# Segment sums on VectorE instead of TensorE, and one mean V moved into the first phase, in a two-part sequence kernel

## The chip, the cores and the metric

The kernel runs on one core of a Trainium2 chip. The metric is the device time of one execution in microseconds; lower is better. Each kernel was run several times, and beside runs of the kernel before on the same chip. The spans in the profiles are about 1.7 us shorter than the run times (1241.5 us of span against 1243.15 us for the same run of the kernel before).

## The reference

Two independent parts read inputs of 2048 positions and 1024 channels, and their outputs are put side by side.

```python
def _A_ref(x, ...):                     # a diagonal state space model
    Bu = jnp.einsum('bld,pd->blp', x + 0j, B_bar)
    for t in range(L):
        h = Lam_bar[None, :] * h + Bu[:, t, :]
    ...
def _B_ref(x, mem0, Wq, Wk, Wv, Wo, seg_len):   # attention by segments of 32, with a memory of 8 rows
    for s in range(n_seg):              # 64 segments, 32 heads of 128
        xs = x[:, s * seg_len:(s + 1) * seg_len, :].copy()
        h = jnp.concatenate([mem, xs], axis=1)
        v = jnp.einsum('btd,dhe->bhte', h, Wv)
        ...                             # q, k, softmax, output projection
        mem = o[:, :M, :].copy()        # the memory of the next segment
```

The memory makes part B sequential. The kernel avoids that with a first guess of every segment's memory: attention with equal weights, that is the mean of x over the segment (xbar), times Wv (the "mean V"), times Wo. A test on the chip raises a flag where the guess is not good enough, and a general path then runs.

## The kernel before

The engines have short names: `PE` is TensorE, `V` is VectorE, `S` is ScalarE (ACT), `G` is GpSimd. The profile calls VectorE DVE.

In the **first phase** (up to about 348 us) TensorE alternates between one step of part A (16 matmuls into psU) and one V piece of part B (32 matmuls into psP). There are 32 steps and 32 V pieces; after some steps there is no V piece. VectorE does the work of the steps. ScalarE copies a_g for the steps, makes part of their tables, and takes every V piece out of psP:

```python
    def stage1(self, pc, tb):           # one step of part A
        ...
        u = k.ps("U", (128, 2, TB))     # two psU buffers
        ...                             # 16 matmuls into u
        V.tensor_tensor(pr[:], u[:]..., view(t3, ...), ALU.mult)
        V.tensor_tensor(w, w, pr[:, :, 1, :], ALU.add)
        for j in range(2):
            V.tensor_tensor_scan(w[:, j, :], rb, w[:, j, :], ...)
            S.activation(g[:, j, :], w[:, j, :], ACT.Copy)     # ACT waits for the scan
        ...                             # GpSimd: the carry to the next step
        V.tensor_tensor(n[:], g[:]..., view(r3, ...), ALU.mult)  # DVE waits for a_g
        V.tensor_tensor(h[:], n[:, :, 0, :], n[:, :, 1, :], ALU.add)
```

The sums over the segments came from TensorE: 128 small matmuls of x rows with an indicator matrix, and VectorE scaled them out of PSUM.

```python
    def sum_x(self, tmp):
        ...                             # x rows loaded again, 128 at a time
        p = k.ps("R")
        for t in range(TT):             # TT = 16
            xr = xrs.pop(t)
            for c in range(KC):         # KC = 8
                o = c * NSEG + 4 * t
                k.PE.matmul(p[:, o:o + 4], xr[:, c * 128:(c + 1) * 128], k.ind[:], start=True, stop=True)
            load(t + 4)
            yield
        ...                             # xbar = p / L, three VectorE instructions
```

The loop of the first phase places them, and the mean V of a head block (`og`, 32 matmuls of 128x63 from Wv and xbar) comes after the last V piece of that block, for blocks 3 to 7. Blocks 2, 0 and 1 follow in the second phase:

```python
            for kind, pc, q in order[1:]:
                ...
                if kind == "v":
                    b.v_x(pc, q, wv[pc])           # one V piece
                    if q == 3:
                        if pc >= 3:
                            b.og(pc, wv[pc])       # needs xbar
                        n = (pc + 2) if pc + 2 < PC else (2, 0)[pc + 2 - PC]
                        wv[n] = b.load_wv(n)
                    continue
                ...
                if n == 1:
                    next(sx)
                if n >= 3:
                    for _ in range(2):
                        next(sx, None)             # two of the 16 groups of sums
                a.stage1(pc, q)                    # one step of part A, number n
                if q == 2 and pc + 1 < PC:
                    a.tables(pc + 1)               # tables: DVE and ACT by turns
```

TensorE's instructions of this phase stay in the order of the program (`keep_in_program_order`), so a matmul that waits holds up everything behind it.

Of the kernel before, what the change touches and what calls it, by code (L numbers as in the profile page):

```python
# [8 lines left out]
FP32 = mybir.dt.float32  # L9
BF16 = mybir.dt.bfloat16  # L10
I32 = mybir.dt.int32
ACT = mybir.ActivationFunctionType
ALU = mybir.AluOpType
AX = mybir.AxisListType
# [10 lines left out]
PC = 8; TB = 512; NB = 4  # L25
# [72 lines left out]
def consts(k):  # L98
    nc, V, G = k.nc, k.V, k.G
    c = k.cst  # L100
    k.ident = c.tile([128, 128], BF16, name="ident")
    G.memset(k.ident[:], 1.0)
    G.affine_select(out=k.ident[:], in_=k.ident[:], compare_op=ALU.is_equal, fill=0.0, base=0,
                    pattern=[[-1, 128]], channel_multiplier=1)
    k.ones = c.tile([128, 1], BF16, name="ones")
    V.memset(k.ones[:], 1.0)
    k.hpb = c.tile([128, 1], FP32, name="hpb")
    k.hpe = c.tile([128, 1], FP32, name="hpe")
    V.memset(k.hpb[:], HALF_PI)
    k.S.activation(k.hpe[:], k.hpb[:], ACT.Exp)  # L110
    k.ind = c.tile([128, 4], BF16, name="ind")
    G.memset(k.ind[:], 0.0)
    for j in range(4):
        G.memset(k.ind[32 * j:32 * j + 32, j:j + 1], 1.0)


def masks(k):
# [45 lines left out]
class PartA:  # L163
# [97 lines left out]
        for i, w in enumerate((self.Cim, self.Cre)):  # L261
            self.k.SP.dma_start_transpose(self.CT[:, i, :, cols], w[cols, :])

    def stage1(self, pc, tb):

        k = self.k; V, S, G, PE = k.V, k.S, k.G, k.PE
        if tb == 0:
            self.carry = None
        t3, r3 = self.tabs
        u = k.ps("U", (128, 2, TB))  # L270
        for i in range(2):
            for c in range(KC):
                PE.matmul(u[:, i, :], self.bt[:, i, c, :], self.xT[:, c, tb * TB:(tb + 1) * TB], start=(c == 0), stop=(c == KC - 1))
        pr = self.wp.tile([128, 2, 2, TB], FP32, name="a_pr", bufs=2)
        V.tensor_tensor(pr[:], u[:].unsqueeze(1).to_broadcast([128, 2, 2, TB]),  # L275
                        view(t3, [[TB + 1, 2], [TB + 1, 2], [1, TB]]), ALU.mult)
        w = pr[:, :, 0, :]
        V.tensor_tensor(w, w, pr[:, :, 1, :], ALU.add)
        rb = self.rr[:, pc:pc + 1].to_broadcast([128, TB])
        ini = self.carry  # L280
        g = self.wp.tile([128, 2, TB], BF16, name="a_g", bufs=2)
        for j in range(2):
            V.tensor_tensor_scan(w[:, j, :], rb, w[:, j, :], 0.0 if ini is None else ini[:, j:j + 1], ALU.mult, ALU.add)  # L283
            S.activation(g[:, j, :], w[:, j, :], ACT.Copy)
        if tb < NB - 1:
            nx = self.wp.tile([128, 2], FP32, name="a_nx", bufs=2); tt = self.wp.tile([128, 2], FP32, name="a_tt", bufs=2)
            for j in range(2):
                G.tensor_scalar(tt[:, j:j + 1], w[:, j, TB - 1:TB], t3[:, 1, TB:TB + 1], None, ALU.mult)  # L288
                G.tensor_scalar(nx[:, j:j + 1], w[:, 1 - j, TB - 1:TB], t3[:, 2 - 2 * j, TB:TB + 1], None, ALU.mult)
            G.tensor_tensor(nx[:], nx[:], tt[:], ALU.add)  # L290
            self.carry = nx
        n = self.wp.tile([128, 2, 2, TB], BF16, name="a_n", bufs=1)
        h = self.wp.tile([128, 2, TB], BF16, name="a_h", bufs=2)
        V.tensor_tensor(n[:], g[:].unsqueeze(1).to_broadcast([128, 2, 2, TB]), view(r3, [[TB, 2], [TB, 2], [1, TB]]), ALU.mult)
        V.tensor_tensor(h[:], n[:, :, 0, :], n[:, :, 1, :], ALU.add)
        k.SP.dma_start(self.hs[tb][:, pc, :, :], h[:])
# [48 lines left out]
class PartB:  # L345
# [77 lines left out]

    def sum_x(self, tmp):

        k = self.k
        xrs = {}

        def load(t):
            if t < TT:  # L430
                xrs[t] = tmp.tile([128, D], BF16, name="b_xr", bufs=4)
                k.SP.dma_start(xrs[t][:], self.x[0][t * 128:(t + 1) * 128, :])
        for t in range(4):
            load(t)
        yield
        p = k.ps("R")
        for t in range(TT):
            xr = xrs.pop(t)
            for c in range(KC):
                o = c * NSEG + 4 * t  # L440
                k.PE.matmul(p[:, o:o + 4], xr[:, c * 128:(c + 1) * 128], k.ind[:], start=True, stop=True)
            load(t + 4)
            yield
        pv = p[:].rearrange("p (c s) -> p c s", c=KC)
        ms = tmp.tile([128, KC], FP32, name="b_ms", bufs=1)
        k.V.tensor_reduce(ms[:], self.m0T[:], AX.X, ALU.add)
        k.V.tensor_scalar(self.xbar[:], pv, 1.0 / L, None, ALU.mult)
        k.V.tensor_tensor(ms[:], ms[:], pv[:, :, 0], ALU.add)
        k.V.tensor_scalar(self.xbar[:, :, 0], ms[:], 1.0 / L, None, ALU.mult)
        yield  # L450

    def load_wv(self, hb):
# [108 lines left out]
    def v_mem(self, hb, w=None):  # L561
        k = self.k
        w = w or self.load_wv(hb)
        p = k.ps("P")
        for h in range(4):
            for c in range(KC):
                k.PE.matmul(p[:, h * NM:(h + 1) * NM], w[:, c, h * 128:(h + 1) * 128], self.memT[:, c, :], start=(c == 0), stop=(c == KC - 1))
        vm = self.vmp.tile([128, 4, 128], BF16, name="b_vm", bufs=1)
        k.copy("v", vm[:, :, 0:NM], p[:, 0:4 * NM].rearrange("p (h n) -> p h n", h=4))
        if hb > 1:  # L570

            k.V.memset(vm[:, :, NM:128], 0.0)  # L572
            k.SP.dma_start(self.vmt[hb][:], vm[:].rearrange("p h n -> p (h n)"))
            yield
            s = self.next_st()[:].rearrange("p i h e -> p (i h e)")[:, 0:576].rearrange("p (h e) -> p h e", h=4)
            k.V.memset(s[:, :, E:EW], 1.0)
            for h in range(4):
                k.SP.dma_start_transpose(s[:, h, 0:E], self.vmt[hb][:, h * 128:(h + 1) * 128])
            yield
            k.SP.dma_start(self.vx[hb][64:64 + NMX, :].rearrange("n (h e) -> n h e", h=4), s[0:NMX, :, 0:EW])  # L580
            self.store_t(hb, s[:, :, 0:EW])
            yield
        yield
        pt = k.ps("P", (128, 1024), BF16)
        for h in range(4):
            k.PE.transpose(pt[0:NM, h * 128:(h + 1) * 128], vm[:, h, 0:NM], k.ident[:])
        st = self.next_st()
        k.copy("v", st[0:NM, 0, :, 0:E], pt[0:NM, 0:512].rearrange("p (h e) -> p h e", h=4))
        sv = st[:, 0, :, :].rearrange("p h e -> p (h e)")
        k.SP.dma_start(self.vx[hb][64:64 + NMX, :], sv[0:NMX, :])  # L590
        self.store_t(hb, st[:, 0, :, :])
        yield
# [427 lines left out]
def kernel_main(tc, A_x, A_Lre, A_Lim, A_Bre, A_Bim, A_Cre, A_Cim, A_logdt, A_Dskip, B_x, B_mem0, B_Wq, B_Wk, B_Wv, B_Wo, out,  # L1020
                force=False, dbg=None):
    with ExitStack() as ctx:
        k = K(tc, ctx)
        k.dbg = dbg
        nc = k.nc
        a = PartA(k, A_x, A_Lre, A_Lim, A_Bre, A_Bim, A_Cre, A_Cim, A_logdt, A_Dskip, out)
# [12 lines left out]
        with pool("p1x", "right") as p1x, pool("p1", "right", 1) as p1:  # L1039
# [28 lines left out]
            for kind, pc, q in order[1:]:  # L1068
                if loads and kind == "v":
                    for o, n in loads.pop(0):  # L1070
                        o.load_x(n)
                if kind == "v":
                    b.v_x(pc, q, wv[pc])
                    if q == 3:
                        if pc >= 3:
                            b.og(pc, wv[pc])
                        n = (pc + 2) if pc + 2 < PC else (2, 0)[pc + 2 - PC]
                        wv[n] = b.load_wv(n)
                    continue
                a.tabs, a.bt = tabs[pc], bts[pc]  # L1080
                n = 4 * pc + q
                if q == 2 and pc + 1 < PC:
                    a.load_b(pc + 1)
                    bts[pc + 1], a.bt = a.bt, bts[pc]
                if pc >= 4 and q == 1:
                    a.load_c(pc - 4)
                if n == 1:
                    next(sx)
                if n >= 3:
                    for _ in range(2):  # L1090
                        next(sx, None)
                a.stage1(pc, q)
                if q == 2 and pc + 1 < PC:
                    a.tables(pc + 1)
                    tabs[pc + 1] = a.tabs
                if n == 12:
                    masks(k)
                    check_consts(k)
                if n == 14:
                    b.fill(p1)  # L1100
# [8 lines left out]
        with pool("p2h", "right") as p2h, pool("p2", "right") as p2:  # L1109
# [3 lines left out]
            b.wog = []  # L1113
            a.load_h(1, nc.scalar)
            for i, _ in enumerate(s2):
                if i in (1, 4, 7):
                    n = (2, 0, 1)[(i - 1) // 3]
                    b.og(n, wv[n], "O")
                    if n == 2:
                        wv[1] = b.load_wv(1)  # L1120
                if i in (3, 7, 11, 15):
                    b.load_wog((3, 7, 11, 15).index(i), p2)
                if i in (9, 11, 13, 15, 17, 19, 21, 22):
# [143 lines left out]
```

## Time and profile before

| | before |
|---|---|
| time, median of 3 runs | 1243.16 us (1243.0 to 1243.27) |
| profiled span, granted clock | 1241.5 us, 1.000 |
| TensorE busy | 1230.8 us, 99% |
| VectorE busy, whole span / 40 to 140 us | 54% / 84% |
| DMA | 178.42 MB |

The page of the kernel before: busy time by engine, and the shares of the chain that ended last.

```profile
PE 1230.8 (99%) x8246; PEld 658.8 (53%) x8318; DVE 667.8 (54%) x1254; ACT 266.6 (21%) x695; POOL 278.1 (22%) x442
...
PE 96%; DMA 3%; issue 0%; SPq 0%; DVE 0%
```

TensorE bounds the kernel. Time is won only by taking work from it.

TensorE's timeline of the kernel before. Columns: start in us, duration in us, engine, line, operation, output and inputs, shape, count.

```profile
67.49 0.54 PE L68 MATMUL psR<-ind,b_xr 128*128 128x4 bf16 x16
67.89 3.61 PE L68 MATMUL psU<-a_xT,a_bt 128*128 128x512 bf16 x16
71.34 7.07 PE L68 MATMUL psP<-b_wv,b_xe 128*128 128x512 bf16 x31
...
170.84 1.10 PE L68 MATMUL psR<-b_xbar,b_wv 128*128 128x63 bf16 x32
171.77 3.62 PE L68 MATMUL psU<-a_xT,a_bt 128*128 128x512 bf16 x15
```

No line has a bracket, so TensorE waits for nothing. The durations overlap, so costs are read from start to start: 0.40 us for 16 sum matmuls (67.49 to 67.89), 3.45 us for a step's psU, 6.91 us for a V piece (71.34 to 78.25, where the next group of sums begins), and 0.93 us for the 32 matmuls of a mean V. The first mean V is asked for at 170.84 us.

VectorE's timeline of the kernel before, one ordinary step and the scaling of the sums. The bracket is the idle time before an instruction and what ended it.

```profile
96.72 2.46 DVE L283 TENSOR_TENSOR_SCAN a_pr<-a_rr,a_nx,a_pr 128x512 f32<-128x512 f32 x2
99.88 1.22 DVE L294 TENSOR_TENSOR a_n<-a_g,a_tabh 128x2048 bf16<-128x2048 bf16 x1 [0.70 <-ACT a_g L284]
...
103.82 2.29 DVE L275 TENSOR_TENSOR a_pr<-psU,a_tabf 128x2048 f32<-128x2048 f32 x1 [2.00 <-PE psU L68]
...
138.98 0.68 DVE L447 TENSOR_SCALAR b_xbar<-psR 128x512 bf16<-128x512 f32 x1
```

A step has two idle places: 0.70 us where VectorE waits for ACT's a_g, and in most steps up to 2 us where it waits for the next psU. The change wants to fill both. The sums are scaled at 139 us, 31 us before they are needed.

Busy time by stretch, kernel before. Columns: stretch, its length, then busy time and instructions of PE, PEld, DVE, ACT and POOL, the granted clock, DMA share, GB/s.

```profile
40.00:140.00 100.00, 99.42 (x568) 46.99 (x577) 84.38 (x75) 40.19 (x71) 23.67 (x40) 1.00 0.67 188
140.00:240.00 100.00, 99.47 (x510) 46.35 (x519) 91.93 (x82) 43.85 (x77) 22.86 (x37) 1.00 0.47 130
```

### The profile page before, as it was taken

Reading aid. Unit: us, or ns where it says so; the run is one execution under the profiler, and the core shown is the slowest. Engines: PE = TensorE matmul, PEld = TensorE weight load, DVE = VectorE, ACT = ScalarE, POOL = GpSimd, SP = SyncE. Lnnn points to the kernel's source line nnn. Section 1 sums busy time; section 2 is a strip of 40 time slices with the busy share of each in tenths; the row PEclk is TensorE's granted clock in tenths of the full one; section 3 lists DMA queues with packets and bytes.
Section 4 is the critical chain, followed back from the end, with each engine's and each line's share of the span. In section 5 each row is a group of like instructions: output and inputs, shape, how many; then the busy total and the mean of one; then the engine's idle time right before and its main releaser. Section 6 shows DMA issues by size and latency. Waiting matters only on the chain.

```text
span 1241.5 us, 20294 instructions
## 1 busy us (share of the span) xinstructions
PE 1230.8 (99%) x8246; PEld 658.8 (53%) x8318; DVE 667.8 (54%) x1254; ACT 266.6 (21%) x695; POOL 278.1 (22%) x442
## 2 busy tenths in 40 slices
PE   9999999999999999999999999999999999999998
PEld 4444444444455555556565656556565654445444
DVE  4688899998811124666666666666666641001000
ACT  5344344443310000111112121212111210000000
POOL 4111331222322330232223232222322220000000
PEclk9999999999999999999999999999999999999999
DMA  9965444644898834675464554545564279507000
GB/s 251 267 184 158 131 120 133 156 143 118 221 325 247 267 109 106 150 200 139 109 153 108 126 135 114 131 94 140 112 146 101 59 198 252 113 17 154 17 17 27
DMA packets 322357, 178.42 MB, mean 144 GB/s; under 512 B 144666, under 2 KB 307660, under 8 KB 322260
## 3 DMA queue, kind: packets, MB, share of 16 engines
q1 hardware_dynamic: 300164, 149.53, 49.4%
q10 hardware_dynamic: 21072, 24.38, 6.0%
q0 software_dynamic: 1024, 3.17, 0.7%
q8 instruction: 66, 1.08, 0.4%
q14 instruction: 31, 0.25, 0.1%
HBM read 89.14 MB, written 53.96 MB: 115 GB/s over the span
## 4 chain that ended last, share of the span: by engine, by line
PE 96%; DMA 3%; issue 0%; SPq 0%; DVE 0%
PE psP L68 80%; PE psU L68 9%; PE psS L68 3%; PE psO L68 2%; DMA b_v<-b_vx 2%; PE psR L68 2%; DMA b_wv<-in_B_Wv_dram 1%; SPq L68 0%; DVE b_ost L95 0%; DVE b_vm L572 0%
## 5 line engine op out<-in xcount | busy, mean ns | idle before, releaser
L68 PE MATMUL psP<-b_xe,b_wq 128*128 128x480 bf16 (+1 forms) x1280 | 247.5, 343 | 0.1
L68 PE MATMUL psP<-b_xe,b_wk 128*128 128x480 bf16 (+1 forms) x1280 | 247.5, 343 | 0.0
L68 PE MATMUL psP<-b_wv,b_xe 128*128 128x512 bf16 (+2 forms) x1033 | 223.5, 372 | 1.2 <-DMA b_wv<-in_B_Wv_dram 0.4
L694 POOL TENSOR_TENSOR b_m<-b_e,maskB 99x396 bf16<-99x396 bf16 (+1 forms) x160 | 134.4, 840 | 337.0 <-ACT b_e L693 337.0
L693 ACT ACTIVATE b_e<-psS 99x396 bf16<-99x396 f32 (+3 forms) x208 | 91.3, 441 | 531.7 <-PE psS L68 523.4
L68 PEld LDWEIGHTS <-b_wk 128*128 128x128 bf16 x1280 | 119.2, 98 | 94.2
L68 PEld LDWEIGHTS <-b_xe 128*128 128x128 bf16 x1056 | 101.8, 98 | 119.6 <-issue 0.7
L68 PEld LDWEIGHTS <-b_wq 128*128 128x128 bf16 x1280 | 118.5, 98 | 87.7
L95 DVE CAST b_k<-psP 128x480 bf16<-128x480 f32 (+1 forms) x192 | 97.3, 528 | 100.9 <-PE psP L68 100.9
L95 DVE CAST b_q<-psP 128x480 bf16<-128x480 f32 (+1 forms) x192 | 97.3, 528 | 92.2 <-PE psP L68 90.9
L68 PEld LDWEIGHTS <-b_ol 128*128 128x128 bf16 x864 | 84.3, 98 | 94.4
L68 PE MATMUL psU<-a_xT,a_bt 128*128 128x512 bf16 x493 | 113.9, 379 | 1.1
L68 PE MATMUL psP<-t,a_hl 128*128 128x512 bf16 x496 | 112.1, 379 | 0.8
L95 DVE CAST b_ost<-psP 128x512 bf16<-128x512 f32 (+1 forms) x17 | 11.5, 676 | 177.6 <-PE psP L68 176.6
L68 PE MATMUL psP<-wo,b_ol 128*128 128x512 bf16 (+1 forms) x440 | 91.9, 364 | 0.4
L68 PE MATMUL psP<-t,b_ol 128*128 128x512 bf16 x408 | 91.7, 379 | 0.4
L288 POOL TENSOR_SCALAR a_tt<-a_pr,a_tabf 128x1 f32<-128x1 f32 x48 | 34.0, 709 | 242.6 <-DVE a_pr L283 242.6
L93 ACT ACTIVATE b_vst<-psP 128x512 bf16<-128x512 f32 x126 | 72.0, 588 | 72.4 <-PE psP L68 65.1
L711 DVE TENSOR_TENSOR b_ob<-psO,b_accR 99x384 bf16<-99x384 f32 x160 | 86.0, 554 | 2.2
L275 DVE TENSOR_TENSOR a_pr<-psU,a_tabf 128x2048 f32<-128x2048 f32 x32 | 73.0, 2282 | 16.2 <-PE psU L68 14.5
L68 PEld LDWEIGHTS <-a_bt 128*128 128x128 bf16 x512 | 49.2, 98 | 57.6
L68 PEld LDWEIGHTS <-a_hl 128*128 128x128 bf16 x512 | 49.0, 98 | 56.7
(204 smaller groups left out, 969.7 us busy)
## 6 DMA issues: line engine op xcount, KB each, us to landing
b_v<-b_vx SPq DMA_DIRECT2D x16, 1122.0 KB
b_wv<-in_B_Wv_dram SPq DMA_DIRECT2D x16, 1024.0 KB
b_vx<-b_vst ACTq DMA_DIRECT2D x24, 544.0 KB
b_on<-b_ob SPq DMA_DIRECT2D x15, 720.0 KB
a_hs<-a_h SPq DMA_DIRECT2D x32, 256.0 KB
b_wog<-in_B_Wo_dram SPq DMA_DIRECT2D x4, 2048.0 KB
b_wq<-in_B_Wq_dram SPq DMA_DIRECT2D x16, 512.0 KB
b_wk<-in_B_Wk_dram SPq DMA_DIRECT2D x16, 512.0 KB
```

Source lines behind the costliest of these rows:

```text
L68: r = f(*a, **kw)
L93: self.S.activation(out, in_, ACT.Copy)
L95: self.V.tensor_copy(out, in_)
L275: V.tensor_tensor(pr[:], u[:].unsqueeze(1).to_broadcast([128, 2, 2, TB]), view(t3, [[TB + 1, 2], [TB + 1, 2], [1, TB]]), ALU.mult)
L288: G.tensor_scalar(tt[:, j:j + 1], w[:, j, TB - 1:TB], t3[:, 1, TB:TB + 1], None, ALU.mult)
L693: k.S.activation(e[:, a:b, :, 0:n], s[0:GW, a:b, :, 0:n], ACT.Exp, scale=float(E) ** -0.5, accum_out=self.accE[0:GW, j:j + 1])
L694: k.G.tensor_tensor(mv[:, a:b, :, 0:n], e[:, a:b, :, 0:n], mask[0:GW, :, 0:n].unsqueeze(2).to_broadcast([GW, b - a, 2, n]), ALU.mult)
L711: V.tensor_tensor(self.ob[:, b0:b0 + n, :], o[0:GW, 0:n, 0:E], r.unsqueeze(2).to_broadcast([GW, n, E]), ALU.mult)
```

## The change

The intent: VectorE adds up the segments from xe, the transposed x that already lies on the chip, in its idle places, and TensorE loses 128 matmuls. As xbar is then there earlier, block 2's mean V comes directly after its last V piece, which saves a reload of Wv. One transposing DMA takes the place of four in late head blocks. The diff, cut to its core:

```diff
-    def stage1(self, pc, tb):
+    def stage1(self, pc, tb, between):
 ...                                     # after the scans and the carry:
+        between()
         n = self.wp.tile([128, 2, 2, TB], BF16, name="a_n", bufs=1)
 ...
     def sum_x(self, tmp):
-        ...                             # loads of x, 128 matmuls into psR (cut)
+        k = self.k; V = k.V
+        xs = tmp.tile([128, KC, NSEG], FP32, name="b_xr", bufs=4)
+        for j in range(TT):
+            r = V.tensor_reduce(xs[:, :, 4 * j:4 * j + 4], self.xe[:, :, 128 * j:128 * j + 128].rearrange("p c (s t) -> p c s t", s=4),
+                                AX.X, ALU.add)
+            k.tc.keep_in_program_order(r)
             yield
 ...                                     # scaling to xbar from xs instead of psR (cut)
-            for h in range(4):
-                k.SP.dma_start_transpose(s[:, h, 0:E], self.vmt[hb][:, h * 128:(h + 1) * 128])
+            k.SP.dma_start_transpose(s[:, :, 0:E], self.vmt[hb][:])
 ...
-                        if pc >= 3:
+                        if pc >= 2:
                             b.og(pc, wv[pc])
-                        n = (pc + 2) if pc + 2 < PC else (2, 0)[pc + 2 - PC]
+                        n = (pc + 2) if pc + 2 < PC else (0, 1)[pc + 2 - PC]
 ...
-                if n == 1:
-                    next(sx)
-                if n >= 3:
-                    for _ in range(2):
-                        next(sx, None)
-                a.stage1(pc, q)
+                a.stage1(pc, q, lambda: next(sx, None))
+                if n < 8:
+                    next(sx)
 ...
-                if i in (1, 4, 7):
-                    n = (2, 0, 1)[(i - 1) // 3]
+                if i in (1, 4):
+                    n = (i - 1) // 3
                     b.og(n, wv[n], "O")
-                    if n == 2:
-                        wv[1] = b.load_wv(1)
```

So steps 0 to 7 carry two reductions each, one between the scans and a_n and one after a_h, each pinned behind the VectorE instruction written before it. The scaling follows in step 8.

More of the change, by code (lines that the diff above doesn't have):

```diff
@@ L110, in consts @@
     k.S.activation(k.hpe[:], k.hpb[:], ACT.Exp)
-    k.ind = c.tile([128, 4], BF16, name="ind")
-    G.memset(k.ind[:], 0.0)
-    for j in range(4):
-        G.memset(k.ind[32 * j:32 * j + 32, j:j + 1], 1.0)
 def masks(k):
@@ L424, in sum_x @@
     def sum_x(self, tmp):
-        k = self.k
-        xrs = {}
-        def load(t):
-            if t < TT:
-                xrs[t] = tmp.tile([128, D], BF16, name="b_xr", bufs=4)
-                k.SP.dma_start(xrs[t][:], self.x[0][t * 128:(t + 1) * 128, :])
-        for t in range(4):
-            load(t)
-        yield
-        p = k.ps("R")
-        for t in range(TT):
-            xr = xrs.pop(t)
-            for c in range(KC):
-                o = c * NSEG + 4 * t
-                k.PE.matmul(p[:, o:o + 4], xr[:, c * 128:(c + 1) * 128], k.ind[:], start=True, stop=True)
-            load(t + 4)
+        k = self.k; V = k.V
[4 more added lines that the diff above has]
+            k.tc.keep_in_program_order(r)
             yield
-        pv = p[:].rearrange("p (c s) -> p c s", c=KC)
+        e = NSEG - 4
         ms = tmp.tile([128, KC], FP32, name="b_ms", bufs=1)
-        k.V.tensor_reduce(ms[:], self.m0T[:], AX.X, ALU.add)
-        k.V.tensor_scalar(self.xbar[:], pv, 1.0 / L, None, ALU.mult)
-        k.V.tensor_tensor(ms[:], ms[:], pv[:, :, 0], ALU.add)
-        k.V.tensor_scalar(self.xbar[:, :, 0], ms[:], 1.0 / L, None, ALU.mult)
+        V.tensor_reduce(ms[:], self.m0T[:], AX.X, ALU.add)
+        V.tensor_tensor(xs[:, :, e], xs[:, :, e], ms[:], ALU.add)
+        V.tensor_scalar(self.xbar[:, :, 2:NSEG - 2], xs[:, :, 0:e], 1.0 / L, None, ALU.mult)
+        V.tensor_scalar(self.xbar[:, :, 0:2], xs[:, :, e:e + 2], 1.0 / L, None, ALU.mult)
+        V.tensor_scalar(self.xbar[:, :, NSEG - 2:NSEG], xs[:, :, e + 2:NSEG], 1.0 / L, None, ALU.mult)
         yield
```

## The prediction

> **What bounds the kernel.** TensorE. The page's busy table has PE busy 1230.8 of 1241.5 us and the chain of waits is 96% PE; the granted clock is full. In the first phase (up to about 348 us) the tensor engine's timeline has no holes: a step is 16 matmuls into psU (3.45 us) and 32 of V (6.91 us), 10.36 us. VectorE comes next: in the busy table by stretch it works 15.5 of 20 us at 40 to 80 us and 17 to 19 of 20 us from 80 to 340 us. So only tensor work taken away counts, and only as long as VectorE does not begin to hold TensorE.
>
> **What is removed.** 128 matmuls of 128x4 with their weight loads (psR from ind and b_xr). Their own durations (164 ns) overlap; the timeline shows 0.40 us between the last V matmul and the next psU for each of eight groups of 16 (67.49 to 67.89, 78.25 to 78.65, ...): 3.2 us, all on the critical path. Also 16 loads of x rows (4 MB), one 1 MB reload of Wv, and three of four transposing DMAs per late head block: TensorE waits 0.4 us for Wv in the whole run, so these are worth about nothing. The mean V of head block 2 moves from the second phase to the first; its 32 matmuls cost 0.93 us in both places.
>
> **What is added.** 16 reductions of 128x1024 to 128x32 on VectorE. The Trainium skill, "VectorE: DVE Perf Modes", section "The perf-mode tier table", gives tensor_reduce only its slowest mode, one element per cycle. The trace agrees: the reductions at the end take 361 ns for 208 elements and 875 ns for 704, 1.04 ns per element plus 0.15 us. Estimate from these: 1.2 us each, about 1.15 back to back, 18 us in all, against about 1 us removed (the scaling of the sums out of PSUM).
>
> **Does it fit?** Each reduction is pinned behind the vector instruction written before it: one goes into the 0.7 us wait for ACT's a_g, one after a_h in the wait for psU. The vector timeline before has 7 x 0.7 us and 1.8 + 1.6 + 2.0 + 1.2 + 2.0 us idle from 40 to 120 us: 13.5 us, for 18 us of work. So a step of 8.8 us becomes about 10.2, plus tables every fourth step, against 10.36 on TensorE, which skips a V piece at step 6. VectorE falls behind: I put the end of step 7 at about 125 us (119.9 before), and the sums scaled at 127 at the earliest, about 132 if the step 8 products go first. TensorE, sped up by then, reaches the new mean V of block 2, directly after V piece (2,3), at about 122.8 us. It needs xbar and is kept in order: a stall of 4 to 10 us, not recovered later, for TensorE is full elsewhere. Before, the first mean V was asked for at 170.8 us, 31 us after xbar.
>
> **Time.** 1243.2 - 3.2 + about 7 = 1247 us; 1239.9 if the vector engine is in time after all. Range 1239.5 to 1252. Faster by over 2%: 1%; within 2%: 98%; slower: 1%.
>
> **What would show it.** No matmul psR from b_xr; psU following V at once at 67.5 us. Tensor_reduce x16 at 1.2 us. A hole in TensorE's timeline near 123 to 132 us, ahead of the first matmuls from b_xbar, released by VectorE's xbar. VectorE at 98% or more from 80 to 130 us. DMA some 5 MB less, without effect.
>
> **What would make it wrong.** The scaling being issued ahead of step 8's products, or reductions faster than one element per cycle: then no stall, and about 1240. Or further stalls: psU not freed in time by a lagging VectorE at the double psU near 147 us.

## The result, and the profile after

| | before | after |
|---|---|---|
| time, median of 4 runs | 1243.22 us (1243.0 to 1244.0) | 1250.35 us (1250.24 to 1251.4) |
| ratio after/before, 95% interval | | 1.0058 (1.0041 to 1.0076) |
| profiled span, granted clock | 1241.5 us, 1.000 | 1248.5 us, 0.997 |
| DMA | 178.42 MB | 173.15 MB |

A ratio here and below is the mean time of one kernel's runs over the mean of the other's runs of the same rounds, so it is not quite the ratio of the medians quoted. The change is within 2%, and about 7 us slower.

The page after: busy time and the chain's shares.

```profile
PE 1229.4 (98%) x8119; PEld 656.2 (53%) x8190; DVE 684.9 (55%) x1272; ACT 266.3 (21%) x694; POOL 273.9 (22%) x437
...
PE 90%; DVE 5%; DMA 4%; issue 1%; SPq 0%; DVEq 0%
```

VectorE now stands in the chain with 5%, against 0% before. TensorE's timeline after shows where:

```profile
67.64 3.62 PE L68 MATMUL psU<-a_xT,a_bt 128*128 128x512 bf16 x16
...
111.51 1.89 PE L68 MATMUL psP<-b_wv,b_xe 128*128 128x512 bf16 x8 [0.53 <-ACT b_vst L93]
113.23 3.62 PE L68 MATMUL psU<-a_xT,a_bt 128*128 128x512 bf16 x16
116.68 7.19 PE L68 MATMUL psP<-b_wv,b_xe 128*128 128x512 bf16 x31
130.38 1.87 PE L68 MATMUL psR<-b_xbar,b_wv 128*128 128x63 bf16 x32 [6.51 <-DVE b_xbar L436]
132.47 4.20 PE L68 MATMUL psU<-a_xT,a_bt 128*128 128x512 bf16 x15 [0.22 <-issue]
136.50 7.07 PE L68 MATMUL psP<-b_wv,b_xe 128*128 128x512 bf16 x32
```

The sum matmuls are gone. At 123.9 us TensorE comes to the new mean V of block 2 and stands still for 6.51 us until VectorE's last piece of xbar. VectorE's timeline after, towards the end of the sums:

```profile
121.20 2.28 DVE L271 TENSOR_TENSOR a_pr<-psU,a_tabf 128x2048 f32<-128x2048 f32 x1
123.40 1.22 DVE L291 TENSOR_TENSOR a_n<-a_g,a_tabh 128x2048 bf16<-128x2048 bf16 x1
124.53 1.22 DVE L274 TENSOR_TENSOR a_pr<-a_pr 128x1024 f32<-128x1024 f32 x1
125.67 0.68 DVE L292 TENSOR_TENSOR a_h<-a_n 128x1024 bf16<-128x1024 bf16 x1
126.27 1.21 DVE L426 TENSOR_REDUCE b_xr<-b_xe 128x32 f32<-128x1024 bf16 x1
127.40 2.33 DVE L279 TENSOR_TENSOR_SCAN a_pr<-a_rr,a_pr 128x512 f32<-128x512 f32 x2
129.65 0.17 DVE L433 TENSOR_TENSOR b_xr<-b_xr,b_ms 128x8 f32<-128x8 f32 x1
129.74 0.40 DVE L434 TENSOR_SCALAR b_xbar<-b_xr 128x480 bf16<-128x480 f32 x1
130.06 0.17 DVE L435 TENSOR_SCALAR b_xbar<-b_xr 128x16 bf16<-128x16 f32 x1
130.14 0.20 DVE L436 TENSOR_SCALAR b_xbar<-b_xr 128x16 bf16<-128x16 f32 x1
```

No line has a bracket: VectorE is never idle here, it is behind. The last reduction ends at 127.5 us and the sums are scaled at 130.3 us. Step 8's products, addition and scans (L271, L274, L279) go ahead of the scaling.

Busy time by stretch after, with two short stretches behind the hole.

```profile
40.00:140.00 100.00, 92.31 (x441) 42.69 (x449) 96.77 (x88) 37.95 (x66) 16.37 (x35) 0.97 0.53 144
...
130.30:132.50 2.20, 1.90 (x33) 1.84 (x34) 2.00 (x4) 0.72 (x2) 2.20 (x3) 0.50 0.25 63
132.40:136.50 4.10, 4.03 (x15) 1.69 (x15) 3.16 (x6) 0.63 (x1) 0.30 (x2) 0.80 0.49 132
```

VectorE rose from 84.38 to 96.77 of 100 us. The granted clock is 0.50 in the first 2.2 us after the hole and 0.80 in the next 4.1. The mean V took 2.09 us from start to start (130.38 to 132.47) instead of 0.93, and the next psU 4.03 instead of 3.45: 1.74 us lost on top of the hole. The Trainium skill, "TensorE: Matmul & The Clock Gate", Part 1 (the section on the clock gate), says that the array's clock falls to half after an idle window of about 3.4 us and comes back after a busy one. This trace agrees, with 0.50 after 6.51 us of idleness: in stretches of half a microsecond the clock is still 1.00 up to 127.0 us, falls to 0.50 within the stretch from 127.0 to 127.5, some 3.4 us after TensorE stopped, and is back in the one from 134.0 to 134.5. It does not agree on the idle time that it takes: in e8, below, holes of 2.02 and 2.94 us were enough.

The same points of TensorE's timeline in both kernels give a ledger of the whole difference:

| point (start, us) | before | after | difference | what came in since the row above |
|---|---|---|---|---|
| psU after the first sums | 67.89 | 67.64 | −0.25 | sums −0.40; +0.15 from earlier |
| psU of step 8 | 114.78 | 113.23 | −1.55 | sums 5 × −0.40; +0.7 a wait for ACT at 111 us |
| psU of step 9 | 125.55 | 132.47 | +6.92 | sums −0.40; hole 6.51 and 0.28 of matmul tail; mean V 2.09 |
| psU of step 10 | 136.31 | 143.41 | +7.10 | sums −0.40; +0.58 slow clock |
| last mean V of the first phase | 347.23 | 354.34 | +7.11 | nothing |
| first matmul with Wq | 471.47 | 478.25 | +6.78 | −0.93 mean V moved away; +0.6 wait for Wv of block 1 |

The spans differ by 7.0 us. So nearly all of the loss is made in one place, within 20 us of the run (116 to 136 us).

### The profile page after: what moved, and what is told of

Read it like the earlier page. It is cut to its first block, busy times and chain, and to the rows that moved or that the text cites. A ratio compares the mean times of both kernels' runs of the same rounds, so it can differ in the third digit from the quotient of the medians. Undisturbed runs are those within 1.5% of the kernel's fastest.

```text
span 1248.5 us, 20001 instructions
## 1 busy us (share of the span) xinstructions
PE 1229.4 (98%) x8119; PEld 656.2 (53%) x8190; DVE 684.9 (55%) x1272; ACT 266.3 (21%) x694; POOL 273.9 (22%) x437
## 2 busy tenths in 40 slices
DMA packets 318437, 173.15 MB, mean 139 GB/s; under 512 B 143819, under 2 KB 305789, under 8 KB 318341
## 3 DMA queue, kind: packets, MB, share of 16 engines
q0 software_dynamic: 1024, 3.17, 0.7%
## 4 chain that ended last, share of the span: by engine, by line
PE 90%; DVE 5%; DMA 4%; issue 1%; SPq 0%; DVEq 0%
PE psP L68 76%; PE psU L68 8%; PE psS L68 3%; PE psO L68 2%; DMA b_v<-b_vx 2%; DMA b_wv<-in_B_Wv_dram 2%; PE psR L68 2%; DVE a_pr L279 1%; DVE a_pr L271 1%; DVE b_xr L426 1%; DVE a_pr L274 1%; DVE a_n L291 0%; DVE a_h L292 0%; SPq L68 0%; DVE a_tabh L241 0%
## 5 line engine op out<-in xcount | busy, mean ns | idle before, releaser
L271 DVE TENSOR_TENSOR a_pr<-psU,a_tabf 128x2048 f32<-128x2048 f32 x32 | 73.1, 2283 | 10.0 <-PE psU L68 8.0
```

The source lines that it names most:

```text
L271: V.tensor_tensor(pr[:], u[:].unsqueeze(1).to_broadcast([128, 2, 2, TB]), view(t3, [[TB + 1, 2], [TB + 1, 2], [1, TB]]), ALU.mult)
```

## The experiments

My theory at this point: only the early mean V of block 2 costs time; with it elsewhere, the change would be worth its 3.2 us (about 1240.5 us). Its rival: VectorE's lag costs time in itself, whoever asks for xbar. Differences between kernels that ran on different chips are good to about half a microsecond: the medians of the kernel before lay between 1243.22 and 1243.64.

### e1: the mean V of block 2 back in the second phase

```diff
-                        if pc >= 2:
+                        if pc >= 3:
-                        n = (pc + 2) if pc + 2 < PC else (0, 1)[pc + 2 - PC]
+                        n = (pc + 2) if pc + 2 < PC else (2, 0)[pc + 2 - PC]
-                if i in (1, 4):
-                    n = (i - 1) // 3
+                if i in (1, 4, 7):
+                    n = (2, 0, 1)[(i - 1) // 3]
 ...
+                    if n == 2:
+                        wv[1] = b.load_wv(1)
```

> The change with the mean V of block 2 put back into the second phase (with its reload of Wv), all else kept, so all 16 reductions are still on VectorE in the same places. Theory (the hole comes only from block 2's mean V asking for xbar 6.5 us too early): no wait of TensorE for b_xbar, no slow clock near 130 us, 3.2 us of matmuls gone, about 0.7 us lost again where ACT empties psP late near 111 us: 1240.5 us, range 1239.8 to 1241.3. Rival (a lagging VectorE itself slows the first phase, by late freeing of psU and psP): 1245 or more, with waits of psU for VectorE. Rival (the new order of Wv loads or the single transposing DMA costs): Wv order undone here, so if this is 1240 and the next kernel is not, it is the Wv order.

Measured: 1243.90 us (1243.76 to 1244.2) against 1243.42 before, ratio 1.0005 (0.9992 to 1.0019). The hole is gone, and the time falls by 6.4 us. But the gain that I expected is missing: the kernel is level with before. The line of TensorE's waits in e1 that is new (columns: waiter, what it waited for, us in total, times, longest):

```profile
PE psP L68 <- ACT b_vst L93: 3.2, 4, 1.0
```

The second of these four in TensorE's timeline in e1:

```profile
141.69 3.61 PE L68 MATMUL psP<-b_wv,b_xe 128*128 128x512 bf16 x16 [0.72 <-ACT b_vst L93]
```

ScalarE's timeline in e1 before that matmul:

```profile
132.58 0.60 ACT L93 ACTIVATE b_vst<-psP 128x512 bf16<-128x512 f32 x1
138.69 0.63 ACT L280 ACTIVATE a_g<-a_pr 128x512 bf16<-128x512 f32 x1 [5.51 <-DVE a_pr L279]
139.87 0.63 ACT L280 ACTIVATE a_g<-a_pr 128x512 bf16<-128x512 f32 x1 [0.55 <-DVE a_pr L279]
140.51 0.63 ACT L233 ACTIVATE a_k<-a_fr 128x513 f32<-128x513 f32 x1
141.05 0.58 ACT L93 ACTIVATE b_vst<-psP 128x512 bf16<-128x512 f32 x1
```

ACT is idle for 5.51 us until VectorE's scan, then does its two a_g and a table instruction, and only then the copy that frees psP, at 141.05 us. That copy's V piece (127.20 to 134.27 us in TensorE's timeline) had long been done: its fourth group stood in psP for nearly 7 us, because the copy was queued behind work that waits for VectorE. The Trainium skill, "TensorE: Matmul & The Clock Gate", section "Architectural detail", says under "Engine queue depths" that ACT and DVE are "strict FIFO". The trace agrees: the ready copy did not pass the waiting a_g. The rival has its mechanism here. VectorE's lag reaches TensorE through ACT's queue and the three psP buffers. My theory was half right.

### e2: the mean V two V pieces later

```diff
+                    if (pc, q) == (3, 1):
+                        b.og(2, wv[2])
+                        wv[4] = b.load_wv(4)
-                    if q == 3:
-                        if pc >= 2:
+                    if q == 3 and pc != 2:
+                        if pc >= 3:
```

> The change with the mean V of block 2 still in the first phase but two V pieces later, after V piece (3,1), near 142 us on TensorE, with the load of Wv block 4 moved behind it. xbar was ready at 130.3 us. Theory: no hole, no slow clock; 1240.5 us (0.7 us near 111 us and up to 0.6 us for Wv block 1 in the second phase stay), range 1239.8 to 1241.5. Rival (doing block 2 in the first phase costs by itself, or its new Wv order does): more than 1 us slower than the kernel with block 2 put back.

Measured: 1244.76 us (1243.5 to 1245.58), ratio 1.0009 (0.9995 to 1.0023). As expected there is no wait for xbar. The size is missed for e1's reason: the waits for ACT's b_vst sum to 2.3 us (4 of them), and a wait for Wv of block 1 in the second phase adds 1.6 us.

### e3: the scaling ahead of step 8's products

```diff
+                if n == 8:
+                    next(sx)
                 a.stage1(pc, q, lambda: next(sx, None))
```

> The change with the scaling of the sums written ahead of step 8's stage instead of inside it; on VectorE it is then issued right after the 16th reduction, ahead of step 8's scans. Theory (TensorE waits for the end of this one chain on VectorE): xbar about 2 us sooner, hole about 4.5 us instead of 6.5, 1248.2 us, range 1247.3 to 1249. [...] Rival (the hole is not released by xbar but by something else on VectorE at that point): no change, 1250.3.

Measured: 1249.59 us (1249.28 to 1250.04), ratio 1.0050 (1.0036 to 1.0063). The hole became 1.2 us shorter. TensorE's timeline in e3:

```profile
129.18 1.86 PE L68 MATMUL psR<-b_xbar,b_wv 128*128 128x63 bf16 x32 [5.34 <-DVE b_xbar L435]
131.27 4.81 PE L68 MATMUL psU<-a_xT,a_bt 128*128 128x512 bf16 x15 [0.22 <-issue]
135.92 4.26 PE L68 MATMUL psP<-b_wv,b_xe 128*128 128x512 bf16 x19
```

The mean V took 2.09 us and the psU 4.65 from start to start: 2.36 us lost to the slow clock, more than after the longer hole of the change (1.74). The granted clock shows why: it falls to 0.50 and comes back in the same half microseconds as in the change (127.0 to 127.5 and 134.0 to 134.5 us), and as e3's matmuls began 1.2 us sooner, 1.2 us more of them ran at half speed, which costs 0.6 us. Some of the scaling instructions were still issued among step 8's work, so the edit moved less than I meant it to, and the time lies outside the range I gave. The direction was right, and the order of the last instructions is worth about 0.8 us, not the whole hole.

### e4: six reductions before step 0

```diff
             sx = b.sum_x(p1)
+            for _ in range(6):
+                next(sx)
 ...
-                    next(sx)
+                    next(sx, None)
```

> The change with six of the 16 reductions written ahead of step 0, where VectorE was idle (6 to 7 us near 28 to 35 us); the scaling then ends in step 5, before 110 us, and block 2's mean V stays where the change put it. Theory (too much work on VectorE between 40 and 127 us, not the place of the mean V as such): no hole, 1240.5 us, range 1239.8 to 1241.8; a later start of step 0's products (about 43 us instead of 40) without effect on TensorE. Rival (the place of the mean V costs for another reason): 1247 or more.

Measured: 1242.07 us (1241.91 to 1243.7), ratio 0.9991 (0.9977 to 1.0005). The mean V of block 2 stands where the change put it, and there is no hole: with less left to do, VectorE is in time. It is still 1.6 us above what I expected and outside my range, and TensorE waits 2.2 us for b_vst (2 times) in the profiled execution, which was the slowest of the five (1243.70 us).

### e5: the kernel before with one transposing DMA

```diff
-            for h in range(4):
-                k.SP.dma_start_transpose(s[:, h, 0:E], self.vmt[hb][:, h * 128:(h + 1) * 128])
+            k.SP.dma_start_transpose(s[:, :, 0:E], self.vmt[hb][:])
```

> The kernel before with only the single transposing DMA in place of four for each of the six late head blocks. Theory: off the critical path, 1243.2 us, within 0.3 us. Rival (it costs or saves on the queue that also loads V for the attention): a difference of over 0.5 us.

Measured: 1243.54 us (1243.37 to 1243.88) against 1243.31, ratio 1.0001 (0.9988 to 1.0015). As expected, this part is worth nothing here.

### e6: the last four reductions done twice

```diff
             k.tc.keep_in_program_order(r)
+            if j >= 12:
+                r = V.tensor_reduce(...)          # the same again
+                k.tc.keep_in_program_order(r)
```

> The change with the last four of the 16 reductions done twice, same result. Theory (the hole is VectorE's lag): 4 x about 1.12 us more on VectorE ahead of the scaling, so the hole grows from 6.5 to about 11 us and the time to 1254.8 us, range 1253.8 to 1256; the slow clock after the hole costs the same 1.7 us. Rival (the hole is set by something else, such as POOL, ACT or a DMA): 1250 to 1251.

Measured: 1255.20 us (1253.82 to 1255.85), ratio 1.0092 (1.0076 to 1.0107): a hit. TensorE's timeline in e6:

```profile
134.92 1.86 PE L68 MATMUL psR<-b_xbar,b_wv 128*128 128x63 bf16 x32 [10.89 <-DVE b_xbar L440]
```

Four more reductions lengthened the hole from 6.51 to 10.89 us, 1.10 us each, almost their full duration. VectorE has no idle place left there, and the hole is its lag. The time rose by 4.85 us, 0.5 more than the hole: the clock came back only at 139.5 to 140.0 us, so that more of the matmuls after the hole ran at half speed than in the change.

### e7: two reductions early, the others spread over ten steps (on e1)

```diff
             sx = b.sum_x(p1)
+            for _ in range(2):
+                next(sx)
-                if n < 8:
+                if n < 4:
                     next(sx)
```

> The kernel with block 2's mean V put back, with the 16 reductions spread: two ahead of step 0, two a step in steps 0 to 3, one a step in steps 4 to 9. New theory (a lagging VectorE makes ACT late, because ACT's copies out of psP stand behind a_g in its queue and a_g waits for the scans; TensorE then waits for psP: 3.2 us in four waits in that kernel): with a small lag these waits go, to 0.5 us or less in all, 1240.7 us, range 1240.0 to 1241.5. Rival (the 3.2 us of waits for ACT come from something other than the lag, such as the DMA out of b_vst): 1243 or more, waits as before.

Measured: 1242.20 us (1241.91 to 1242.66) against 1243.62, ratio 0.9988 (0.9974 to 1.0002). The waits for b_vst fall from 3.2 to 1.4 us (2 of them, at 157 and 203 us), and the time by 1.7 us from e1. That is a miss of the 1240.7 us I expected, but the same work, less dense, gives back part of the gain.

### e8: a_g of steps 6 to 16 on GpSimd (on e1)

The idea: if a_g is what stops ACT's queue, then another engine that makes a_g lets the copies through.

```diff
+            if 6 <= 4 * pc + tb <= 16:
+                G.tensor_copy(g[:, j, :], w[:, j, :])
+            else:
+                S.activation(g[:, j, :], w[:, j, :], ACT.Copy)
```

> The kernel with block 2's mean V put back, reductions where the change has them, but the copies a_g of steps 6 to 16 made by GpSimd instead of ACT. Theory as above: nothing that waits for the scans stands ahead of ACT's psP copies any more, so TensorE's waits for b_vst fall from 3.2 us to under 0.6 us although VectorE lags as much or more; 1241 us, range 1240.2 to 1242.2 (a GpSimd copy slower than ACT's 0.63 us may add lag and waits of psU for VectorE). Rival (the lag holds TensorE by psU, or the copies are late for their own sake): no better than 1243.5.

Measured: 1251.52 us (1250.76 to 1252.16), ratio 1.0061 (1.0048 to 1.0075): a miss in the wrong direction. The waits for b_vst grew to 7.2 us. ScalarE's timeline in e8:

```profile
131.99 0.63 ACT L242 ACTIVATE a_tabh<-a_tabh 128x512 bf16<-128x512 bf16 x1 [8.15 <-DVE a_tabh L238]
132.53 1.56 ACT L93 ACTIVATE b_vst<-psP 128x512 bf16<-128x512 f32 x3
142.81 0.63 ACT L233 ACTIVATE a_k<-a_fr 128x513 f32<-128x513 f32 x1 [8.72 <-DVE a_fr L230]
143.34 0.58 ACT L93 ACTIVATE b_vst<-psP 128x512 bf16<-128x512 f32 x1
```

With a_g away, the table instructions stand at the head of ACT's queue and wait for VectorE for 8 us and more, with three ready copies behind them. "a_g blocks the queue" was too narrow; any ACT instruction that waits for a late VectorE does. GpSimd's copies (0.6 to 1.5 us each) delayed VectorE's a_n besides.

e8 also shows how little idleness the clock needs. After a TensorE hole of 2.02 us (to 143.97 us) the granted clock was 0.50 from 144.2 to 147.4 us, and after one of 2.94 us (to 218.76) from 219.2 to 222.6; in e4 a hole of 1.99 us left it at 1.00. Each stretch of half clock here lasted about 3.4 us; the one after the change's hole and e3's lasted 6.8 us, e6's and e11's 13.6.

### e9: as e7, with the mean V of block 2 late in the first phase

```diff
+                    if (pc, q) == (3, 2):
+                        b.og(2, wv[2])
+                        wv[4] = b.load_wv(4)
 ...                                     # as in e2: no mean V at q == 3 for block 2
-                if i in (1, 4, 7):
-                    n = (2, 0, 1)[(i - 1) // 3]
+                if i in (1, 7):
+                    n = i // 7
```

> The attempt at a version better than both: reductions spread as above, block 2's mean V in the first phase but after V piece (3,2), near 163 us, and block 1's mean V in the second phase three steps later than in the change, so that its Wv load has landed. Theory: no wait for xbar, none for Wv, those for b_vst 0.5 us or less: 1240.3 us, range 1239.7 to 1241.3, faster than before by 0.2%. If the Wv load of block 4, now issued near 164 us, is late for V piece (4,0) near 185 us, a wait for b_wv shows instead.

Measured: 1242.48 us (1242.26 to 1243.0), ratio 0.9990 (0.9976 to 1.0003). No wait for xbar or for Wv of block 1 is left; 1.8 us of waits for b_vst are (3 of them). That is outside my range (1239.7 to 1241.3): moving the mean V and saving a reload gains nothing over e7.

### e10: no sums at all (on e1; not a valid kernel)

The sums are set to zero and the flag of the test is forced to "good". The comparison with the reference still passed, but a kernel that skips its sums and its own test of them is no version to use; it only shows what VectorE's sums cost.

```diff
-            r = V.tensor_reduce(...)
-            k.tc.keep_in_program_order(r)
+            if j == 0:
+                k.tc.keep_in_program_order(V.memset(xs[:], 0.0))
...
-        V.tensor_copy(self.flag[:], fl[0:1, :])
+        V.memset(self.flag[:], 0)
```

> Wrong result on purpose: the kernel with block 2's mean V put back, the 16 reductions left out (sums set to zero, the flag that would start the exact path held at 0). TensorE does the same work as in that kernel, VectorE 18 us less in the first phase. If the 3.2 us of waits for ACT's psP copies come from VectorE's lag caused by the reductions: they go, and the time is 1240.4 us, range 1239.7 to 1241.0. If they come from TensorE being 3.2 us ahead of a first phase that VectorE and ACT already nearly filled, whoever does the sums: waits of 1 to 3 us stay, 1241.5 to 1243.5.

Measured: 1240.78 us (1240.19 to 1241.45) against 1243.64, ratio 0.9977 (0.9964 to 0.9991): a hit. All of TensorE's listed waits in e10:

```profile
PE psO L68 <- DMA b_v<-b_vx: 1.4, 1, 1.4
PE psR L68 <- DVE hpb L109: 1.3, 1, 1.3
PE psU L68 <- DMA b_xr<-in_B_x_dram: 0.7, 1, 0.7
PE psP L68 <- DMA b_wv<-in_B_Wv_dram: 0.3, 1, 0.3
```

No wait for b_vst is left. With the medians compared across chips, so to about half a microsecond each, this splits the result in three: taking the sums from TensorE −2.9 us (before to e10), the reductions on VectorE +3.1 us (e10 to e1), the early mean V +6.4 us (e1 to after).

### e11: the sums on GpSimd (on e1)

A first form with GpSimd's own reduction along the free axis did not build. This one adds halves five times:

```diff
-            r = V.tensor_reduce(...)
+            G.tensor_tensor(t[:], xv[:, :, :, 0:16], xv[:, :, :, 16:32], ALU.add)     # pinned
+            for m in (8, 4, 2):
+                G.tensor_tensor(t[:, :, :, 0:m], t[:, :, :, 0:m], t[:, :, :, m:2 * m], ALU.add)
+            G.tensor_tensor(xs[:, :, 4 * j:4 * j + 4], t[:, :, :, 0], t[:, :, :, 1], ALU.add)
```

> The kernel with block 2's mean V put back, the sums made by GpSimd in the same places, each as a tree of five additions, right result. VectorE is as free as without sums if GpSimd's work does not slow it. Estimate from a_xd (1024 elements in 2.1 us on GpSimd): 2.5 us a tile, 40 us in all, in its idle time. If the lag of VectorE is the cause and GpSimd does not disturb it: 1240.7 us, range 1239.9 to 1241.5, better than before by 0.2%. If GpSimd's additions lengthen VectorE's instructions or hold up the carry a_nx, which GpSimd also makes: waits of psP or psU again and 1242 to 1246.

Measured: 1258.12 us (1258.0 to 1258.45), ratio 1.0117 (1.0101 to 1.0132): a miss. GpSimd is busy 81.68 of 100 us from 40 to 140 us, and TensorE waits 15.2 us for b_vst. Most of that, one wait of 11.81 us, comes from GpSimd being late with the sums. Its last three took 3.1 us each where I had estimated 2.5, and VectorE stood idle for them ahead of the scaling:

```profile
132.51 0.17 DVE L437 TENSOR_TENSOR b_xr<-b_xr,b_ms 128x8 f32<-128x8 f32 x1 [10.31 <-POOL b_xr L432]
```

ACT's next table instruction then waits for VectorE until 135.93 us, with three copies out of psP behind it. So it is the path of e1 and e8 again, with GpSimd at its head.

GpSimd also slowed VectorE's instructions. VectorE's groups from 40 to 140 us (columns: line, operation, shapes, count, busy us, mean ns, idle before), in the kernel before:

```profile
L275 DVE TENSOR_TENSOR a_pr<-psU,a_tabf 128x2048 f32<-128x2048 f32 x11 | 25.1, 2285 | 11.1 <-PE psU L68 11.1
...
L278 DVE TENSOR_TENSOR a_pr<-a_pr 128x1024 f32<-128x1024 f32 x10 | 12.2, 1224 | 0.3
```

The same groups, and the scans, in e11:

```profile
L271 DVE TENSOR_TENSOR a_pr<-psU,a_tabf 128x2048 f32<-128x2048 f32 x9 | 20.5, 2283 | 4.5 <-PE psU L68 4.5
L279 DVE TENSOR_TENSOR_SCAN a_pr<-a_rr,a_nx,a_pr 128x512 f32<-128x512 f32 x12 | 17.6, 1507 | 2.3 <-POOL a_nx L286 1.8
L274 DVE TENSOR_TENSOR a_pr<-a_pr 128x1024 f32<-128x1024 f32 x9 | 13.3, 1482 | 0.2
```

VectorE's own additions grew from 1224 to 1482 ns in the mean, and the scans from 1270 ns (in before) to 1507 and waited for the carry that GpSimd makes late. The products that read PSUM with one input kept their 2285 ns. The Trainium skill, "GPSIMD Engine Reference", § 1 Specifications, says that GpSimd shares its SBUF interfaces with VectorE, with contention where a DVE instruction has two SBUF inputs. The trace agrees, but not evenly: a_n, which reads a_g and a table from SBUF, rose only from 1225 to 1247 ns. Why is not shown.

### e12: four reductions early and unpinned, the others spread (on e1)

```diff
-            k.tc.keep_in_program_order(r)
+            if j >= 4:
+                k.tc.keep_in_program_order(r)
...
+            for _ in range(4):
+                next(sx)
-                if n < 8:
+                if n < 3:
                     next(sx)
```

> The attempt at the best version: block 2's mean V put back; the first four reductions not pinned and written ahead of step 0, so that they run in VectorE's idle places of the first 15 us (the first 512 rows of x are there by then); two a step in steps 0 to 2, one a step in steps 3 to 8. Against the spread kernel two reductions fewer between 26 and 85 us, so a smaller lag. Theory: waits for ACT's psP copies of 0.7 us or less (1.4 there), 1241.5 us, range 1240.7 to 1242.3, at best the 1240.8 us of the kernel without sums. Rival (what is left there is no matter of the lag's size): 1242.2 again, with the same two waits near 157 and 203 us. A loss of up to 0.4 us at the start, where a reduction may delay the copy of x that the first V pieces need, is possible.

Measured: 1241.84 us (1241.51 to 1242.6) against 1243.41, ratio 0.9989 (0.9976 to 1.0003). It has the lowest median of the correct versions, some 0.1% below before, but the interval touches 1, so it is not clearly faster. Two waits for b_vst remain (156.47 and 203.13 us, 1.2 us in all), the two that my rival had named.

### The runs side by side

The second column is the median time above e10's, the third TensorE's waits for ACT's b_vst:

| kernel | above e10, us | waits for b_vst, us | other |
|---|---|---|---|
| e12 | 1.1 | 1.2 | |
| e4 | 1.3 | 2.2 | |
| e7 | 1.4 | 1.4 | |
| e9 | 1.7 | 1.8 | |
| e1 | 3.1 | 3.2 | |
| e2 | 4.0 | 2.3 | 1.6 wait for Wv |
| e8 | 10.7 | 7.2 | half clock twice, 3.4 us each |
| e11 | 17.3 | 15.2 | half clock for 4.3 us after the hole |

Where no other loss is listed, the waits for b_vst account for the time within 0.2 us, except in e4. But the waits are those of one profiled execution, and e4's took 1243.70 us, 2.9 above e10, so that they do not explain more than was lost there. Taken against the times of the profiled executions, the losses listed for e1, e2, e4, e7, e9 and e12 agree within 0.7 us. In e8 and e11 the half clock adds half its length: 7.2 + 3.4 = 10.6 and 15.2 + 2.1 = 17.3. What would remove the two last waits of e12 stays open.

## Why the prediction was right, point by point

The predicted class and range held: 1250.35 us lies inside 1239.5 to 1252, 3.3 us above the 1247 predicted. That it held owes something to its width: the losses that I had not foreseen, listed below, add up to 3.2 us and all go one way, and the range ended 1.65 us above the result.

- **What bounds the kernel, and the 3.2 us removed.** Right. The ledger finds eight times −0.40 us, and e10 gives −2.9 us for the whole.
- **The reductions at 1.2 us each.** Right: 1.196 us in the median, 16 of them. From 361 ns for 208 elements to 1196 for 1024 is 1.02 ns per element, close to the 1.04 of the prediction and so to the one element per cycle of the Trainium skill, "VectorE: DVE Perf Modes", "The perf-mode tier table".
- **VectorE does not fit.** Right. I put the end of step 7, with its last reduction, at about 125 us and the scaling between 127 and 132; they came at 127.5 and 130.3. VectorE was busy 96.77 of 100 us from 40 to 140, and 49.5 of 50 from 80 to 130 (predicted at 98% or more; in before 44.1 of 50), and e6 shows that each further reduction delays xbar by nearly its duration.
- **A stall of 4 to 10 us ahead of block 2's mean V.** Right: 6.51 us, asked for at 123.9 us (predicted 122.8), released by VectorE's xbar. The early mean V cost 6.4 us net, by e1. One way out that I had named would not have helped: with the scaling moved ahead (e3) the hole was still 5.34 us, for the last reduction alone ended at 126.6 us, 2.8 us after TensorE had stopped.
- **Fewer DMA bytes without effect.** 5.3 MB less moved. e5 confirms it for the transposing DMA; the removed loads were not tested alone.
- **The mean V costs 0.93 us in both places.** The step that failed in size. In its new place it started on a half-speed clock and took 2.09 us, and the next psU 0.58 more: 1.74 us that the sum did not have.
- **"For TensorE is full elsewhere."** 0.7 us of wait for ACT at 111 us, and 0.6 us for Wv of block 1 in the second phase, are also missing from the sum. The sum predicted −3.2 + 7 = +3.8 us. Measured: −3.2 sums, +6.8 hole with its tail, +1.74 slow clock, +0.7, +0.6 and +0.15 early in the run, together +6.8 against 7.0 us of span.
- **"1239.9 if the vector engine is in time after all."** Wrong as a counterfactual, and the range did not show it. I treated the xbar stall as the only way from VectorE's lag to TensorE, apart from psU at the double step. e1 has no stall for xbar, and its reductions still cost 3.1 us, through ACT's in-order queue and the psP buffers. The wait for psU that I named as a risk is not among TensorE's waits. In the change itself the hole covered most of this: TensorE stood still while VectorE caught up, so only 0.53 us of b_vst wait is left there.

## What to carry to other kernels

Work moved from a full engine to one that is "54% busy" is free only while the second engine keeps its slack in that very stretch; read its busy time by stretch, and count what it must finish before the first instruction that needs it. An engine that falls behind can hold the full engine without any direct dependency: look for a third engine that serves both in order, and for the buffers it frees. A hole of a few microseconds in TensorE costs more than its length, for the first matmuls after it run at half clock, and shortening it can gain less than was cut off (in e3 1.2 us of hole, 0.8 us of time).

## What the Trainium skill lacked or had wrong

One statement was contradicted, the first below. The rest is what it lacked:

- "TensorE: Matmul & The Clock Gate", Part 1: its table lets the clock fall to half after an idle window of about 3.4 us. In e8's profiled execution it fell after holes of 2.02 and 2.94 us; in e4's it did not after one of 1.99. How much idleness is enough is not shown.
- The same Part 1: its cost of a hole is for short bursts of matmuls between waits for DMA, and there is none for a single hole in a full kernel. Here a hole of 6.51 us cost 1.74 us more by the half clock, and one of 5.34 us cost 2.36 us.
- "VectorE: DVE Perf Modes", "The perf-mode tier table": the speed of tensor_reduce, but no fixed cost; the page's fixed terms elsewhere are those of other instructions. Here 361, 875 and 1196 ns for 208, 704 and 1024 elements: about 0.15 us plus 1.0 ns per element.
- "GPSIMD Engine Reference", § 1: the contention, but not its size for two busy streams of instructions. Here GpSimd at 82% busy lengthened VectorE's 128x1024 f32 additions from 1224 to 1482 ns in the mean, left products with a PSUM input at 2283, and lengthened a_n, with two SBUF inputs in bf16, only from 1225 to 1247.
- No page has the path found here, from a late VectorE over ACT's strict order and PSUM buffers to TensorE: 3.2 us of waits in e1 and 7.2 us in e8, with no wait of TensorE for VectorE itself in that phase.
